# V's weights in one transfer ahead of the last block of x, and block 0's two V sums ahead of block 1's first, in a fused attention and gated MLP kernel

## The chip, the cores and the metric

The kernel runs on one core of a Trainium2 chip. The metric is the device time of one execution in microseconds (us). It is given as the median of several runs; the profile comes from one further execution, whose own time stands beside its span.

A core has five engines with a queue of instructions each: TensorE (PE in the profile: matrix products and transposes, results into the accumulation memory PSUM; PEld is its weight load), VectorE (DVE), ScalarE (ACT), GpSimd (POOL) and SyncE (SP), which here only issues transfers. Every engine takes its own instructions in order; between engines, semaphores make one wait for another. Transfers run on 16 DMA engines that all queues share.

## What is computed

One layer over 2048 rows of width 640 in bf16: a layer norm, whose result feeds both a sliding window attention (32 heads of 20, window 256) and a gated MLP of width 1536; both results are added to the input.

```python
def _A_ref(x, wqkv, wo):
    H = 32; Dh = D // H; W = 256
    qkv = ((x @ wqkv).reshape(B, S, 3, H, Dh)).transpose(2, 0, 3, 1, 4)
    q, k, v = qkv[0], qkv[1], qkv[2]
    scores = jnp.einsum("bhqd,bhkd->bhqk", q, k) * (Dh ** -0.5)
    mask = (idx[:, None] - idx[None, :] >= 0) & (idx[:, None] - idx[None, :] < W)
    p = _softmax(jnp.where(mask[None, None], scores, -1e9), axis=-1)
    o = jnp.einsum("bhqk,bhkd->bhqd", p, v)
    return o.transpose(0, 2, 1, 3).reshape(B, S, D) @ wo

def _B_ref(x, w_gate, w_up, w_down):
    h = _sigmoid(x @ w_gate) * (x @ w_up)
    return h @ w_down

xn = _layernorm(x)
return x + _A_ref(xn, A_wqkv, A_wo) + _B_ref(xn, B_w_gate, B_w_up, B_w_down)
```

## The kernel before

The 2048 rows are four chunks (c = 0 to 3) of 512, and a chunk is four blocks (s) of 128 rows. Width 640 is five slices (d) of 128. For a chunk the kernel needs xnT, the normalized rows turned so that the 640 features lie on the partitions; from it come Q and K (L324), V (L353), and gate and up (L447, L454).

The order of the work is written out by hand: each engine runs what the program issues to it, in that order. The change lies in the opening, which handles chunk 0 block by block, in two places, and in one later load.

**The loads at the top (L162 to L169).** SyncE issues, in this order: rows of block 0, 1 and 3 of x (`load_rows`, 160 KB each), the first half of V's weights (`load_v(0)`, columns 0 to 319 of 640, 400 KB in runs of 640 bytes), block 2 of x, the second half of V's weights, then Q's and K's weights (`load_wqkv`, 800 KB each in runs of 1280 bytes). Behind them on the same queue come the first gate and up weights (L183 on). The tiles of Q's and K's weights have six slices, of which `load_wqkv` fills 1 to 5, since a later step packs them into 0 to 4; V's tile has five. `load_wqkv` is called for Q and K alone, so its `1:` is fixed.

**The normalization of chunk 0.** Blocks 0 and 3 take their statistics on VectorE (`ln_half`, `ln_mv`, L252 and L258), the root on ScalarE (`root`, L644), and `norm` on VectorE (L648, L271). Blocks 1 and 2 take mean and root on ScalarE (`mean_act` L654, `root_act` L659 and L660) and the rest on VectorE (`norm_act`, L664 and L665).

**The transposes.** `transpose_rows(s, copy)` (L277) turns the five slices of a block on TensorE and copies them out of PSUM into xnT (L278): block 0 in two pieces on ScalarE, the others in one piece on VectorE.

**The V sums.** `project_v(c, s, hf)` (L353) is five products, one per slice, of a block's xnT with one half (hf) of V's weights, 128 by 320 out. In the code v01 is block 0, half 1, and v10 block 1, half 0. `copy_v` (L362) casts a sum into the V tile in two pieces of 64 rows. The order on TensorE is: transposes of 0; `keep_busy` of 512 and 128 columns; transposes of 1; v00; v10; transposes of 3; v01; v11; v30; transposes of 2; v31; v20; v21; then Q's and K's projections (`g_qk(0)`). `keep_busy` (L226) multiplies constants into a PSUM tile that nobody reads.

**The down weights.** `load_wd` (L195) loads w_down's twelve slices in five transfers: three, three, two, two and two slices. It is called while TensorE works on chunk 0's gate and up, behind the loads `turn_wo` (L205) and ahead of the stores of chunk 1's Q and K (L332), on SyncE's queue.

Everything after the opening is a fill order computed when the program is built: attention steps of a chunk with gate, up, Q, K, V, down and output work of this and the next chunk between them. The change leaves that order alone.

Of the kernel before, what the change touches and what calls it, by code (L numbers as in the profile page):

```python
# [9 lines left out]
P = 128  # L10
S = 2048
D = 640
# [4 lines left out]
FC = F // P  # L17
CW = 512
# [7 lines left out]
HALF = 320  # L26
# [67 lines left out]
def kernel(  # L94
# [11 lines left out]
    nc = tc.nc  # L106
# [35 lines left out]
    wqkv = [const.tile([P, DC + (part != "v"), D], BF16, name="w" + part) for part in "qkv"]  # L142
    wqkv_r = A_wqkv.rearrange("(c p) n -> p c n", p=P)
# [4 lines left out]

    ones = nc.const_aps.tensor(1.0, [P, CW], BF16)
    def load_wqkv(part):  # L150
        nc.sync.dma_start(out=wqkv[part][:, 1:, :], in_=wqkv_r[:, :, part * D:(part + 1) * D])

    xc[0] = xp.tile([P, SBC, D], BF16, name="xc")

    def load_rows(s, queue):
        queue.dma_start(out=xc[0][:, s, :], in_=xr[:, s, :])  # L156

    def load_v(hf):
        a = hf * HALF
        nc.sync.dma_start(out=wqkv[2][:, :, a:a + HALF], in_=wqkv_r[:, :, 2 * D + a:2 * D + a + HALF])  # L160

    load_rows(0, nc.sync)  # L162
    load_rows(1, nc.sync)
    load_rows(3, nc.sync)
    load_v(0)
    load_rows(2, nc.sync)
    load_v(1)
    load_wqkv(0)
    load_wqkv(1)  # L169

    scratch = {w: tc.dram_tile([H * 32, CW], BF16, name="s" + w) for w in "qk"}
# [22 lines left out]

    def load_wd():  # L195
        wd_r = B_w_down.rearrange("(c p) d -> p c d", p=P)
        for lo, hi in ((0, 3), (3, 6), (6, 8), (8, 10), (10, FC)):
            nc.sync.dma_start(out=wd[:, lo:hi, :], in_=wd_r[:, lo:hi, :])

    wo_i = tc.dram_tile([HG, NG * DH, D], BF16, name="wo_i")  # L200
# [22 lines left out]
    def keep_busy(widths):  # L223
        ps = ps_d.tile([P, CW], FP32, name="pwarm", tag="d")
        for n in widths:
            nc.tensor.matmul(ps[:, 0:n], lhsT=ones[:, 0:P], rhs=ones[:, 0:n], start=True, stop=True)  # L226
# [22 lines left out]
    def ln_half(c, s, a, stats=None):  # L249
        if a == 0:  # L250
            stats = lnp.tile([P, 2, nc.vector.BN_STATS_DIM], FP32, name="stats")
        nc.vector.bn_stats(out=stats[:, a, :], in_=xc[c][:, s, a * HALF:(a + 1) * HALF])  # L252
        return stats

    def ln_mv(stats, mv=None):
        if mv is None:
            mv = lnp.tile([P, nc.vector.BN_AGGR_DIM], FP32, name="mv")
        nc.vector.bn_aggr(out=mv, in_=stats)  # L258
        return mv
# [14 lines left out]
    def transpose_rows(s, copy, lo=0, hi=DC):  # L274
        pt = ps_h.tile([P, DC, P], BF16, name="pt", tag="h")
        for d in range(lo, hi):
            nc.tensor.transpose(pt[:, d, :], xns[0][:, s, d * P:(d + 1) * P], ident)  # L277
        copy(out=xnT[0][:, lo:hi, s * P:(s + 1) * P], in_=pt[:, lo:hi, :])  # L278
# [71 lines left out]
    def project_v(c, s, hf, home=ps_d, tag="d"):  # L350
        ps = home.tile([P, CW], FP32, name="pv", tag=tag)
        for d in range(DC):
            nc.tensor.matmul(ps[:, 0:HALF], lhsT=xnT[c][:, d, s * P:(s + 1) * P],  # L353
                             rhs=wqkv[2][:, d, hf * HALF:(hf + 1) * HALF],
                             start=(d == 0), stop=(d == DC - 1))
        return ps
# [285 lines left out]
    def root(mv):  # L642
        r = lnp.tile([P, 1], FP32, name="rstd")
        nc.scalar.activation(out=r, in_=mv[:, 1:2], func=SQRT, bias=eps)  # L644
        return r
# [17 lines left out]
    def norm_act(s, xn, neg, r):  # L663
        nc.vector.reciprocal(r, r)  # L664
        nc.vector.tensor_scalar(out=xn, in0=xc[0][:, s, :], scalar1=neg[:, 0:1],  # L665
                                scalar2=r[:, 0:1], op0=ADD, op1=MULT)
# [11 lines left out]
    stats3 = ln_half(0, 3, 0)  # L678
    for lo, hi in ((0, 3), (3, DC)):
        transpose_rows(0, act, lo, hi)  # L680
    keep_busy((CW, P))
    norm_act(1, xn1, neg1, r1)
    mv3 = ln_mv(ln_half(0, 3, 1, stats3))
    transpose_rows(1, dve)
    v00 = project_v(0, 0, 0)
    r3 = root(mv3)
    xn2, neg2 = mean_act(2)
    r2 = root_act(2, xn2, neg2)
# [1 line left out]
    v10 = project_v(0, 1, 0)  # L690
    copy_v(0, 0, 0, v00, dve, (0,))
    transpose_rows(3, dve)
    v01 = project_v(0, 0, 1)
    norm_act(2, xn2, neg2, r2)
    copy_v(0, 0, 0, v00, act, (1,))
    copy_v(0, 1, 0, v10, act)
# [32 lines left out]
    fill.add("x2", later(load_x, 2), 0)  # L729
    fill.add("wo_i", later(turn_wo), 0)  # L730
    fill.add("wd", later(load_wd), 0)
    fill.add("qk1", mix(g_qk(1), norms2, 6, 1, False), 50 * MM)
    fill.add("v1", mix(g_v(1), g_gu(1, 0, 2), 1, 2), 40 * 136 + 2 * GU)
# [111 lines left out]
```

## Time and profile before

| what | before |
|---|---|
| median of 3 runs | 308.35 us (308.08 to 308.82) |
| the profiled execution's own time | 308.19 us |
| its span | 306.5 us |
| granted TensorE clock, mean | 1.00 |
| TensorE busy / VectorE / ScalarE / GpSimd | 299.8 / 177.6 / 198.5 / 177.6 us |
| last share of x's blocks 0, 1, 3, 2 landed | 3.14, 3.56, 4.47, 7.35 us |
| last share of V's first half, second half landed | 6.89, 8.47 us |
| last share of Q's and K's weights landed | 10.69, 12.97 us |
| first V sum / first Q product starts | 6.94 / 13.01 us |

Times inside the span are counted from its start. A transfer counts as landed when the last of the 16 DMA engines has reported its share; the trace keeps these reports, and no printed view shows them. In the profile's lines "xn<-xc" reads "writes xn from xc", "x5" is the number of instructions merged into the line, and the name after the engine is the source line. Starts of products are recorded and their ends are modelled, so two neighbouring lines can overlap a little; the chain of waits, followed back from the last instruction, counts a group from the moment it took over.

### The profile page before, as it was taken

What the parts mean: (1) busy time and instruction counts of PE and PEld (TensorE: products, weight loads), DVE (VectorE), ACT (ScalarE), POOL (GpSimd) and SP (SyncE); (2) the same over time, 40 slices, a digit from 0 to 9 for tenths busy, and PEclk for the clock granted to TensorE, in tenths of its full rate; (3) what the DMA queues carried; (4) which work ended last, traced back from release to release, by engine and by line L of the source; (5) the groups of instructions that cost most, each with busy time, mean ns of one, the idle gap of its engine ahead of it and who ended that gap; (6) DMA issues with size and microseconds to landing.
All of it is one profiled execution on the core that took longest, in us unless ns stands there. A gap on an engine that the chain in (4) does not pass through costs nothing.

```text
span 306.5 us, 9993 instructions
## 1 busy us (share of the span) xinstructions
PE 299.8 (98%) x4279; PEld 164.9 (54%) x4314; DVE 177.6 (58%) x355; ACT 198.5 (65%) x197; POOL 177.6 (58%) x317
## 2 busy tenths in 40 slices
PE   7999999999999999999999999999999999999996
PEld 3654444445657654554557654554546665444775
DVE  5735539879675564496946464483733626372433
ACT  6923877698854649888674647878585547778000
POOL 3174687687982927676682728557382847557000
PEclk9999999999999999999999999999999999999999
DMA  7997987986427052810046212740000210000202
GB/s 204 362 326 255 305 202 214 316 243 217 144 91 170 21 180 70 256 58 2 2 132 130 66 58 83 242 137 0 2 2 2 69 42 25 2 2 2 88 21 68
DMA packets 40174, 36.87 MB, mean 120 GB/s; under 512 B 8992, under 2 KB 39840, under 8 KB 40096
## 3 DMA queue, kind: packets, MB, share of 16 engines
q1 hardware_dynamic: 39264, 35.45, 38.1%
q10 hardware_dynamic: 864, 0.77, 0.9%
q8 instruction: 34, 0.56, 0.7%
q14 instruction: 12, 0.10, 0.1%
HBM read 25.59 MB, written 11.44 MB: 121 GB/s over the span
## 4 chain that ended last, share of the span: by engine, by line
PE 96%; issue 1%; DMA 1%; ACT 1%; DVE 0%; SPq 0%
PE y L468 18%; PE pu L454 17%; PE pg L447 17%; PE pqk L324 14%; PE ps L524 9%; PE pv L353 8%; PE y L475 7%; PE acc L557 6%; DMA xc<-in_A_x_dram 1%; PE pt L277 0%; ACT xn L654 0%; ACT xn L659 0%; DVE xn L665 0%; SPq L156 0%; ACT rstd L660 0%
## 5 line engine op out<-in xcount | busy, mean ns | idle before, releaser
L541 POOL TENSOR_SCALAR_AFFINE_SELECT pT<-pT 64x512 bf16<-64x512 bf16 (+1 forms) x256 | 157.3, 614 | 83.0 <-ACT pT L530 70.6
L530 ACT ACTIVATE pT<-ps 128x2048 bf16<-128x2048 f32 (+1 forms) x76 | 141.0, 1855 | 59.5 <-PE ps L524 52.9
L458 DVE SCALAR_TENSOR_TENSOR h<-th,pu 128x512 bf16<-128x512 f32 x48 | 32.7, 681 | 49.7 <-PE pu L454 44.2
L454 PE MATMUL pu<-xnT,wu 128*128 128x512 bf16 x228 | 59.0, 380 | 0.7 <-issue 0.2
L447 PE MATMUL pg<-xnT,wg 128*128 128x512 bf16 x226 | 58.5, 380 | 0.9 <-issue 0.3
L468 PE MATMUL y<-wd,h 128*128 128x320 bf16 (+2 forms) x396 | 56.6, 295 | 0.0
L468 PEld LDWEIGHTS <-h 128*128 128x128 bf16 x396 | 36.8, 98 | 15.6 <-issue 1.8
L450 ACT ACTIVATE th<-pg 128x512 f32<-128x512 f32 x48 | 28.6, 595 | 15.5 <-PE pg L447 15.4
L447 PEld LDWEIGHTS <-wg 128*128 128x128 bf16 x240 | 22.3, 98 | 25.8 <-issue 2.0
L454 PEld LDWEIGHTS <-wu 128*128 128x128 bf16 x240 | 22.0, 98 | 25.5 <-issue 2.0
L524 PE MATMUL ps<-qT,kT 20*64 20x320 bf16 (+4 forms) x1440 | 32.1, 260 | 0.0
L569 DVE STREAM_TRANSPOSE t<-acc 128x512 f32<-128x512 f32 x32 | 21.1, 697 | 17.2 <-PE acc L557 17.2
L524 PEld LDWEIGHTS <-kT 20*64 20x64 bf16 x1440 | 15.4, 103 | 25.0 <-issue 22.4
L479 DVE SCALAR_TENSOR_TENSOR rows<-y,rows 128x320 bf16<-128x320 f32 x30 | 14.5, 488 | 22.5 <-PE y L475 22.4
L581 DVE TENSOR_TENSOR on<-t,rec 128x320 bf16<-128x320 f32 (+4 forms) x48 | 25.9, 540 | 1.1
L353 PE MATMUL pv<-wv,xnT 128*128 128x320 bf16 x160 | 25.8, 300 | 0.0
L475 PE MATMUL y<-wo,oc 128*128 128x320 bf16 (+2 forms) x165 | 24.2, 295 | 0.0
L324 PE MATMUL pqk<-xnT,wk 128*128 128x512 bf16 x97 | 23.0, 380 | 0.2
L324 PE MATMUL pqk<-xnT,wq 128*128 128x512 bf16 x94 | 22.7, 380 | 0.4 <-issue 0.2
L362 DVE CAST v<-pv 64x320 bf16<-64x320 f32 x29 | 14.1, 486 | 11.8 <-PE pv L353 11.6
L557 PE MATMUL acc<-pT,v 64*32 64x320 bf16 (+4 forms) x1440 | 19.7, 253 | 0.0
L557 PEld LDWEIGHTS <-v 64*32 64x32 bf16 x1440 | 16.2, 91 | 5.8 <-issue 1.6
(53 smaller groups left out, 194.8 us busy)
## 6 DMA issues: line engine op xcount, KB each, us to landing
qT<-sq SPq DMA_DIRECT2D x16, 256.0 KB
kT<-sk SPq DMA_DIRECT2D x16, 256.0 KB
sq<-st SPq DMA_DIRECT2D x20, 128.0 KB
sk<-st SPq DMA_DIRECT2D x20, 128.0 KB
out_dram<-rows SPq DMA_DIRECT2D x15, 160.0 KB
wg<-in_B_w_gate_dram SPq DMA_DIRECT2D x4, 480.0 KB
wu<-in_B_w_up_dram SPq DMA_DIRECT2D x4, 480.0 KB
xc<-in_A_x_dram SPq DMA_DIRECT2D x3, 640.0 KB
```

Of the source, the lines that this page charges most:

```text
L324: nc.tensor.matmul(ps, lhsT=wt[:, m, :], rhs=xnT[c][:, d, :], start=(d == 0), stop=(d == DC - 1))
L353: nc.tensor.matmul(ps[:, 0:HALF], lhsT=xnT[c][:, d, s * P:(s + 1) * P], rhs=wqkv[2][:, d, hf * HALF:(hf + 1) * HALF], start=(d == 0), stop ...
L447: nc.tensor.matmul(pg, lhsT=part(wg, d, f), rhs=xnT[c][:, d, :], start=(d == 0), stop=(d == DC - 1))
L450: nc.scalar.activation(out=th, in_=pg, func=TANH, scale=0.5)
L454: nc.tensor.matmul(pu, lhsT=part(wu, d, f), rhs=xnT[c][:, d, :], start=(d == 0), stop=(d == DC - 1))
L458: nc.vector.scalar_tensor_tensor(out=h, in0=th, scalar=1.0, in1=pu, op0=ADD, op1=MULT)
L468: nc.tensor.matmul(y[:, 0:cut[1] - cut[0]], lhsT=ht[c, f][:, s * P:(s + 1) * P], rhs=wd[:, f, cut[0]:cut[1]], start=(f == 0), stop=False)
L475: nc.tensor.matmul(y[:, 0:cut[1] - cut[0]], lhsT=oc[c, m][:, s * P:(s + 1) * P], rhs=wo[:, m, cut[0]:cut[1]], start=False, stop=(m == DC - 1))
L524: nc.tensor.matmul(ps[a * U:(a + 1) * U, i, col * U:(col + n) * U], lhsT=qk["k", kc, o // GH][32 * i:32 * i + DH, o % GH + a, kb * U:(kb + ...
L530: nc.scalar.activation(out=pt[:, :, 0:width], in_=ps[:, :, 0:width], func=EXP, scale=SCALE)
L541: nc.gpsimd.affine_select(out=view, in_=view, pattern=[[0, HG], [0, n], [sign, U]], compare_op=GE, fill=0.0, base=base, channel_multiplier ...
L557: nc.tensor.matmul(acc[32 * i:32 * i + 32, q * U:(q + n) * U], lhsT=vt[kb][a * U:(a + 1) * U, u, h * VW:h * VW + 32], rhs=pt[a * U:(a + 1) ...
```

## The change

V's weights come in one transfer of 800 KB, in runs of 1280 bytes, issued where their first half was, ahead of block 2 of x; the second transfer goes, and `load_v` with it. `load_wqkv` now serves V too, whose tile it fills from slice 0. `keep_busy` after block 0's transposes has 384 columns in one product instead of 640 in two. v00 stands ahead of the transposes of block 1, and v01 right behind them, ahead of v10. w_down is loaded in six transfers of two slices each. No other instruction is added or removed.

```diff
     def load_wqkv(part):
-        nc.sync.dma_start(out=wqkv[part][:, 1:, :], in_=wqkv_r[:, :, part * D:(part + 1) * D])
+        nc.sync.dma_start(out=wqkv[part][:, int(part < 2):, :], in_=wqkv_r[:, :, part * D:(part + 1) * D])
...
-    def load_v(hf):
-        a = hf * HALF
-        nc.sync.dma_start(out=wqkv[2][:, :, a:a + HALF], in_=wqkv_r[:, :, 2 * D + a:2 * D + a + HALF])
...
     load_rows(3, nc.sync)
-    load_v(0)
+    load_wqkv(2)
     load_rows(2, nc.sync)
-    load_v(1)
     load_wqkv(0)
     load_wqkv(1)
...
-        for lo, hi in ((0, 3), (3, 6), (6, 8), (8, 10), (10, FC)):
+        for lo, hi in ((0, 2), (2, 4), (4, 6), (6, 8), (8, 10), (10, FC)):
             nc.sync.dma_start(out=wd[:, lo:hi, :], in_=wd_r[:, lo:hi, :])
...
-    keep_busy((CW, P))
+    keep_busy((3 * P,))
     norm_act(1, xn1, neg1, r1)
     mv3 = ln_mv(ln_half(0, 3, 1, stats3))
+    v00 = project_v(0, 0, 0)
     transpose_rows(1, dve)
-    v00 = project_v(0, 0, 0)
+    v01 = project_v(0, 0, 1)
     r3 = root(mv3)
...
     transpose_rows(3, dve)
-    v01 = project_v(0, 0, 1)
     norm_act(2, xn2, neg2, r2)
```

## The prediction

> **What bounds the kernel.** First the page's busy time by engine and the chain that ended last, by engine.
>
> ```profile
> PE 299.8 (98%) x4279; PEld 164.9 (54%) x4314; DVE 177.6 (58%) x355; ACT 198.5 (65%) x197; POOL 177.6 (58%) x317
> ...
> PE 96%; issue 1%; DMA 1%; ACT 1%; DVE 0%; SPq 0%
> ```
>
> TensorE works in 98% of the 306.5 us span and is 96% of the chain. So the question is what the change does to TensorE's own row of work. The waits of TensorE hold three entries with another engine or a queue behind them: 0.8 us before its first instruction, 0.5 and 0.4 us ahead of the first two groups of transposes; the rest is "issue". After 6.5 us nothing makes it wait, so what the opening loses or wins arrives at the end one for one. Next the chain in order of time, there (start us, us, what):
>
> ```profile
> 5.99 0.46 DVE xn L665
> 6.44 0.05 issue
> 6.49 0.45 PE pt L277 x5
> 6.94 1.51 PE pv L353 x10
> 8.45 0.28 PE pt L277 x5
> 8.73 2.04 PE pv L353 x15
> 10.77 0.28 PE pt L277 x5
> 11.05 2.12 PE pv L353 x15
> 13.17 0.22 PE pqk L324
> ```
>
> Block 1's normalized rows come at 6.44, then TensorE runs without a gap: transposes of 1, two V sums, transposes of 3, three sums, transposes of 2, three sums, Q. One detail: a group of transposes costs 0.28 us, but the first stands at 0.45. The V sum behind it could have started at 6.77 and started at 6.94. The landing records of the trace (each of the 16 DMA engines reports its share; no view prints them) say why: the last share of V's first half came at 6.89. **V's weights are already last there.** So I read the opening's timeline (start us, us, engine, line, operation):
>
> ```profile
> 2.18 0.43 SPq L160 DMA_DIRECT2D wv<-in_A_wqkv_dram  x1
> ...
> 2.66 0.52 SPq L156 DMA_DIRECT2D xc<-in_A_x_dram  x1
> ...
> 3.22 0.43 SPq L160 DMA_DIRECT2D wv<-in_A_wqkv_dram  x1
> ...
> 5.64 0.44 PE L226 MATMUL pwarm<-const-bfloat16-1.0 128*128 128x512 bf16 x2
> 5.73 0.75 ACT L278 COPY xnT<-pt 128x384 bf16<-128x384 bf16 x2
> ...
> 7.00 0.48 DVE L278 COPY xnT<-pt 128x640 bf16<-128x640 bf16 x1
> ...
> 7.37 0.74 ACT L654 ACTIVATE xn<-xc 128x640 bf16<-128x640 bf16 x1
> ```
>
> The two halves are issued 1.04 us apart with x's block 2 between. The windows' DMA share is 0.89 at 3 to 4 us, 0.81 at 4 to 5, then 1.09, 1.06, 1.01, 1.05: from 5 us the DMA engines have no room, and a byte put ahead of another delays it.
>
> **When V is there.** Last landings before: x block 3 at 4.47, V's first half 6.89, x block 2 7.35, V's second half 8.47, wq 10.69, wk 12.97. Now all 800 KB must land before block 0's first V sum, although that sum reads only one half: one transfer, one wait.
> Late bound: the slowest engine keeps its pace and only x block 2 leaves from in front: 8.47 - (7.35 - 6.89) = 8.01.
> Early bound: the pace of wk, an equal transfer with as long rows: engine means of wq and wk are 10.09 and 12.37, so 2.28 us. From x block 3's mean, 4.01, plus 0.30 for the idle shares (1 - 0.89, 1 - 0.81), plus wq's slowest behind its mean, 0.60: 7.19.
> Neither is nearer in kind: the late bound has the place in the queue, the early one the shape. I take the middle, **L = 7.6 us**.
>
> A rule of the Trainium skill points earlier (DMA: Bandwidth & Descriptors, "Rules for kernel authors" and the fixed cost under "Anatomy of one DMA"): coalesce small transfers, since each carries some 2 us of fixed cost. By it, as an estimate, V would land 2 us ahead of the late bound, near 6.0. The trace disagrees: V's second half came 1.12 us behind x block 2 on the slowest engine, half of wq's 2.22, so a queued transfer showed no such fixed part.
>
> **The change part by part.**
> (1) Sum v00 moves ahead of the transposes of block 1. Its other input, block 0's xnT, is copied by 6.48 (5.73 + 0.75), so V decides: start at L + 0.05 (the lag seen at 6.89/6.94) = 7.65 instead of 6.94: +0.71.
> (2) TensorE takes instructions in order, so the transposes of block 1, ready at 6.44, now queue behind v00. They were done ahead of the first V sum and now stand behind it: +0.28.
> (3) Who waits for these: VectorE's copy of block 1 (it began 0.51 after its transposes began, took 0.48), behind it on VectorE block 3's reciprocal and normalization (0.16 + 0.45) and the rest. Counting from L: v00 0.05 to 0.73, transposes of 1 to 1.01, v01 to 1.69, copy of 1 done 1.72, v10 to 2.42; block 3 normalized 2.39; its transposes 2.42 to 2.70; VectorE's cast of half of v00 2.39 to 2.87; copy of 3 done 3.42; v11 to 3.38, so v30 waits some 0.06; block 2's transposes from 4.12. Its x lands at L + 0.46, ScalarE needs 2.14 from there (7.37 to 9.51), VectorE comes to it after the copy of 3 and has it at 4.07: in time by 0.05. v31 to 5.08; copy of 2 done 5.12; v20 waits 0.06. So v01, taken early, covers the copy of block 1, and what is left is +0.12, bounds 0 and 0.4 (a block normalized 0.3 late).
> (4) keep_busy loses 256 columns, 0.11 us by the spacing of 0.22 for 512: nothing, since TensorE then idles for V. Without that idle it would be the -0.11 of the rival below.
> (5) One V issue less on SyncE (0.43): wq and wk go out earlier, but the DMA engines are full and both are needed after 13 us, landed 10.69 and 12.97: nothing.
> (6) w_down in six transfers instead of five, same bytes. SyncE issues them at 53.30 to 56.93 and the Q stores from 57.35 stand behind. One more issue is 0.37 to 0.77 (that line's shortest and longest). Block 1's spreads read those stores; the four pairs of issues end at 75.18, and block 1's first scores come about 81.95; w_down's first reader is at 82.3. Covered by several us: nothing; uncovered, 0.4 to 0.8.
>
> Sum: +0.71 + 0.28 + 0.12 = **+1.11 us**, or L - 6.49. With L at its bounds and (3) at its own: 7.19 - 6.61 = +0.58 up to 8.01 - 6.61 + 0.4 = +1.80. The profiled execution took 308.19 (span 306.5 and 1.7 around it): 309.30. It stands 0.16 below the median of the runs: **309.45**.
>
> **Rivals.**
> *V whole is in time (not slower).* If the longer rows or the single transfer keep the slowest engine from its lag, L is the fastest engine's: 5.45 + 1.13 (its second half behind x block 2: 5.99 to 7.12) = 6.58. V's wait then ends 0.1 after the copy at 6.48 and the gaps at 6.0 to 6.9 are filled by v00: 6.58 - 6.49 = +0.09, and 308.45. If V came still earlier the sum's first three products could start on the first copy, about 6.12, and the run end 0.4 earlier, 307.95. It decides from L below 7.1. For it: the landing spread of 1.44 in V's first half (5.45 to 6.89) may belong to its short rows; wk's is 1.13. Against: it asks the slowest engine to gain over 0.9 us, and spreads over 1.1 stay through wq and wk. With the runs' scatter some of this would read as faster.
>
> *TensorE falls to a lower clock.* It idles from about 5.85 to 7.65. That the array starts slow is seen in this trace though the granted clock reads 1.00: the weight loads of keep_busy at 2.07, 2.50, 2.93, 3.35 are 0.43 apart, later ones 0.22, after some 3.4 us of work. Falling back would cost half of such a stretch, 1.7: 309.45 + 1.7 = 311.15. For it: an idle time four times any after the start. Against: transposes and keep_busy stand right before it, and gaps of 0.46 and 0.41 did nothing. The skill's page (TensorE: Matmul & The Clock Gate, "Why this matters for your kernels") sets the limit at idle gaps of about 3 us; by it 1.8 would be safe and this rival starts only with a wait past 9 us. No run here shows such a gap.
>
> *The sixth w_down transfer is felt.* If block 1's spreads come late in spite of the cover, 0.4 to 0.8 more: near 310.1.
>
> **How the numbers follow.** Chances: forecast 0.70, V in time 0.20, lower clock 0.07, w_down 0.03. The time is the forecast's, **309.45**; its own range is +0.58 to +1.80, 308.9 to 310.15. The range asked for reaches down into the rival of V in time (its +0.09 to +0.58) and leaves out its low end and the lower clock: **308.6 to 310.2**. A measurement here can tell about 0.2%, 0.62 us, from no change. Slower by more: the forecast but for its lowest end (0.64), clock and w_down (0.10): 0.74. Within: the lowest end of the forecast (0.06) and most of the rival (0.14): 0.20. Faster: 0.06, from the rival's 307.95 and scatter.
>
> **What would show it.** Right: TensorE idle about 1.8 us after the second keep_busy, ended by V's weights or named "issue"; v00 near 7.65; V's last landing 7.2 to 8.0 and x block 2's about 0.46 behind; the first Q product near 14.1 instead of 13.01; the chain passing through a V transfer instead of x's block 1; past 14 us the same sequence, shifted. Wrong: v00 starting at 6.5, or a Q start at 13.1 or earlier (V in time); spacings of 0.43 in the first Q products (clock); a first block 1 score shifted by more than Q is (w_down).

## The result, and the profile after

| what | before | changed |
|---|---|---|
| median of 15 runs | 308.20 us (308.08 to 308.82) | 311.76 us (309.53 to 313.97) |
| ratio of the times | | 1.0112, 95% interval 1.0084 to 1.0140 |
| the profiled execution's own time / span | 308.19 / 306.5 us | 310.62 / 308.8 us |
| mean granted TensorE clock, 15 runs of the changed kernel | | 1.00 in 6 runs (309.53 to 311.01), 0.987 to 0.995 in 9 runs (311.64 to 313.97) |
| V's last share landed | 8.47 us (second half) | 8.18 us (whole) |
| first V sum / first Q product starts | 6.94 / 13.01 us | 8.22 / 14.73 us |

The change makes the kernel slower, by 3.6 us in the median against the 1.1 us that were forecast, and its times, which agreed within 0.8 us before, now spread over 4.4 us. The profiled execution is one of the six at full clock, so its trace shows only a part of this. (Lines of the changed kernel below 162 of the old numbering stand five lower: the V sums are L348.) First the page's busy times and the shares of its chain:

```profile
PE 299.5 (97%) x4278; PEld 164.7 (53%) x4313; DVE 177.3 (57%) x355; ACT 198.5 (64%) x197; POOL 177.0 (57%) x317
...
PE 94%; DMA 2%; ACT 1%; issue 1%; POOL 1%; SPq 0%; DVE 0%
```

TensorE does the same work in a longer span, and a transfer has entered the chain. The chain in order of time says which (start us, us, what):

```profile
2.13 0.04 issue
2.18 6.00 DMA wv<-in_A_wqkv_dram
8.18 0.04 issue
8.22 0.84 PE pv L348 x5
9.06 0.28 PE pt L272 x5
9.34 1.44 PE pv L348 x10
10.78 0.28 PE pt L272 x5
11.06 1.44 PE pv L348 x10
12.50 0.28 PE pt L272 x5
12.78 2.12 PE pv L348 x15
14.90 0.22 PE pqk L319
```

Before, the chain ran through x's block 1, ScalarE and VectorE. Now it is SyncE, V's transfer for 6 us, and from 8.22 TensorE without a gap. Behind the first V sum stand the transposes of block 1 that used to be done ahead of it. The waits of TensorE (us in total, times, longest) hold it in two lines:

```profile
PE pv L348 <- DMA wv<-in_A_wqkv_dram: 2.2, 1, 2.2
...
PE ps L519 <- ACT pT L525: 0.2, 1, 0.2
```

The first is the opening: Q starts 1.72 us later. The second is a new wait near 48 us, 0.24 us, of which the prediction said nothing. These two make 1.97 us, and every instruction of ScalarE and VectorE from 60 us to the end stands later by just that. The rest of the span's 2.3 us, 0.35, lies behind VectorE's last instruction, in the stores: 2.69 us from that instruction's end to the span's end, 2.34 before.

### The profile page after: what moved, and what is told of

Read it like the earlier page. It is cut to its first block, busy times and chain, and to the rows that moved or that the text cites. A ratio compares the mean times of both kernels' runs of the same rounds, so it can differ in the third digit from the quotient of the medians.

```text
span 308.8 us, 9992 instructions
## 1 busy us (share of the span) xinstructions
PE 299.5 (97%) x4278; PEld 164.7 (53%) x4313; DVE 177.3 (57%) x355; ACT 198.5 (64%) x197; POOL 177.0 (57%) x317
## 4 chain that ended last, share of the span: by engine, by line
PE 94%; DMA 2%; ACT 1%; issue 1%; POOL 1%; SPq 0%; DVE 0%
PE y L463 17%; PE pu L449 16%; PE pg L442 16%; PE pqk L319 14%; PE ps L519 8%; PE pv L348 8%; PE y L470 7%; PE acc L552 6%; DMA wv<-in_A_wqkv_dram 2%; ACT pT L525 1%; POOL pT L536 1%; SPq L156 0%; PE pt L272 0%; ACT th L445 0%; DVE xn L474 0%
## 5 line engine op out<-in xcount | busy, mean ns | idle before, releaser
L348 PE MATMUL pv<-wv,xnT 128*128 128x320 bf16 x160 | 26.1, 300 | 2.2 <-DMA wv<-in_A_wqkv_dram 2.2
L357 DVE CAST v<-pv 64x320 bf16<-64x320 f32 x29 | 14.1, 485 | 11.8 <-PE pv L348 11.6
L348 PEld LDWEIGHTS <-xnT 128*128 128x128 bf16 x160 | 14.4, 98 | 11.2 <-issue 2.6
```

## Experiments

The theory after the result: two costs. One is the wait for all of V in every execution. The other comes in some executions only: TensorE, idle for over 2 us, is granted a lower clock afterwards. The rivals: the new order costs by itself, the sixth w_down transfer costs, the spread comes from V's landing, or the low clock is chance or belongs to one chip.

**The order alone** (transfers, and w_down, as before):

```diff
-    keep_busy((CW, P))
+    keep_busy((3 * P,))
...
+    v00 = project_v(0, 0, 0)
     transpose_rows(1, dve)
-    v00 = project_v(0, 0, 0)
+    v01 = project_v(0, 0, 1)
...
     transpose_rows(3, dve)
-    v01 = project_v(0, 0, 1)
```

> The kernel before with the changed order on TensorE alone (v00, transposes of block 1, v01, v10; 384 columns of keep_busy); V stays in two transfers around block 2 of x. Theory (the wait for V sets the opening, the order only decides which half is waited for): v00 starts at 6.94 as before, since its half lands at 6.89; v01 then waits for the second half, 8.47, instead of the 7.90 at which TensorE is ready; the first Q product near 14.1 (before 13.01), the run about 1.1 us over before, and TensorE's longest idle time near 1.1 us. If the longest idle time decides whether the clock falls, the mean granted clock stays 1.00 in every run. Rival (the order itself costs, whatever V does): Q near 14.7 and the same slow scatter of times as the changed kernel, 309.5 to 314.

Measured: 309.36 us (308.90 to 309.62, 8 runs), ratio 1.0030 (1.0020 to 1.0040), clock 1.00 in all. TensorE's timeline (start us, us, ... [idle before, what ended it]):

```profile
6.71 0.84 PE L353 MATMUL pv<-wv,xnT 128*128 128x320 bf16 x5 [0.72 <-DMA wv<-in_A_wqkv_dram]
7.39 0.44 PE L277 MATMUL pt<-ident,xn 128*128 128x128 bf16 x5
8.30 1.53 PE L353 MATMUL pv<-wv,xnT 128*128 128x320 bf16 x10 [0.47 <-DMA wv<-in_A_wqkv_dram]
```

As the theory said: each sum waits for its half, Q comes 0.78 later (13.79; 14.1 was expected, but V's second half landed at 8.26 here, not at 8.47), and the narrow spread stays. The 0.24 us near 47 us is here too, so it goes with the order, not with the transfer.

**The single transfer alone** (order, keep_busy and w_down as before):

```diff
-    load_v(0)
+    load_wqkv(2)
     load_rows(2, nc.sync)
-    load_v(1)
```

> The change's single V transfer alone, with the order, keep_busy and w_down of before (transposes of block 1 ahead of v00). Theory: v00 starts when V whole has landed, about 8.2, the transposes of block 1 are done before it and no longer behind it, so Q is at 8.2 + 6.07 = 14.3 against 14.73 in the changed kernel and 13.01 before; TensorE idles 1.3 us there instead of 2.2. If an idle time of 2.2 us is what lets the clock fall, this one keeps 1.00 in most runs and stands 1.3 us over before; if the clock falls here as well, the mean granted clock goes to 0.99 and the times above 311 in many runs. Rival (the order matters more than the load): the time of before within 0.3 us.

Measured: 309.72 us (309.24 to 313.43, 12 runs), ratio 1.0062 (1.0037 to 1.0088). The clock was 0.989 to 0.994 in 3 of 12 runs, and these three are the longest, 311.98 to 313.43; the other nine end at 310.43. In the profile, one at full clock, V landed at 7.84, and its first sum came then:

```profile
6.40 0.45 PE L272 MATMUL pt<-ident,xn 128*128 128x128 bf16 x5 [0.41 <-DVE xn L660]
7.88 1.52 PE L348 MATMUL pv<-wv,xnT 128*128 128x320 bf16 x10 [1.03 <-DMA wv<-in_A_wqkv_dram]
```

Q starts 0.94 late and no wait follows near 47 us. So the transfer alone costs 1.4 us in the median, against 3.6 for the whole change, and the clock falls at times without the new order. The three long runs were not profiled, so how long TensorE idled in them is not known.

**The changed kernel with work in the wait:**

```diff
-    keep_busy((3 * P,))
+    keep_busy((CW,) * 10)
```

> The changed kernel with ten products of 512 columns of keep_busy instead of one of 384 ahead of v00: same wait for V, but TensorE works through it (10 x 0.216 = 2.2 us from 5.65 to 7.85). Theory (the runs above 311 come from a clock that falls after the idle 2.2 us): the mean granted clock is 1.00 in all runs, the times lie between 309.5 and 311, the median about 1.9 us over before, and Q is still near 14.7. Rival (the spread comes from when V lands, or from later waits, not from the clock): the times spread from 309.5 to 314 as without the filler.

Measured: 310.97 us (310.06 to 311.72, 6 runs), ratio 1.0079 (1.0061 to 1.0096), clock 0.999 or 1.00 in all six. The runs near 314 are gone, which fits the clock as their cause; two of the six still end over 311. The median is 2.7 over before and not the 1.9 that were expected. In the profiled execution (311.01) V landed later still, at 8.85, which accounts for this one:

```profile
5.62 2.35 PE L221 MATMUL pwarm<-const-bfloat16-1.0 128*128 128x512 bf16 x10
8.89 0.84 PE L348 MATMUL pv<-wv,xnT 128*128 128x320 bf16 x5 [0.92 <-DMA wv<-in_A_wqkv_dram]
```

**w_down in six transfers alone:**

```diff
-        for lo, hi in ((0, 3), (3, 6), (6, 8), (8, 10), (10, FC)):
+        for lo, hi in ((0, 2), (2, 4), (4, 6), (6, 8), (8, 10), (10, FC)):
```

> The kernel before with w_down in six transfers of two slices, nothing else. Theory (the sixth issue is covered): the time of before within 0.2 us. Rival (it delays the stores of chunk 1's Q and K and what reads them): 0.4 to 0.8 us more, and a wait of TensorE for a transfer or for ScalarE between 45 and 85 us.

Measured: 308.42 us (308.23 to 309.06, 11 runs), ratio 1.0002 (0.9994 to 1.0011). No cost.

**The changed kernel once more**, unedited.

> The changed kernel once more, beside the three others of this job. Theory (an idle TensorE of 2.2 us lets its clock fall in some executions): about half the runs show a mean granted clock of 0.987 to 0.995 and times over 311.5, the others 1.00 and 309.5 to 311; if the profiled execution is one of the former, its granted clock by windows shows a stretch at half speed that begins after the wait for V and lasts 3.5 to 8 us. Rival (the low clock belongs to the chip of the first runs): 1.00 in all runs.

Measured: 312.32 us, 0.995 in 4 of 6 runs (312.26 to 312.96), 1.00 in two (310.27 and 310.43). The profiled execution (312.26, span 310.5) is one of the four:

```profile
8.30 1.49 PE L348 MATMUL pv<-wv,xnT 128*128 128x320 bf16 x5 [2.37 <-DMA wv<-in_A_wqkv_dram]
```

Its windows (start:end length, busy time and instructions of PE, PEld, DVE, ACT and POOL, then the granted clock, the DMA share and GB/s):

```profile
6.00:7.00 1.00, 0.00 (x0) 0.10 (x1) 0.96 (x3) 0.45 (x2) 0.00 (x0) 1.00 1.03 332
7.00:8.00 1.00, 0.00 (x0) 0.00 (x0) 0.04 (x1) 0.29 (x1) 0.00 (x0) 1.00 1.04 383
8.00:9.00 1.00, 0.69 (x3) 0.41 (x3) 0.00 (x0) 0.25 (x1) 0.00 (x0) 0.62 1.07 397
9.00:10.00 1.00, 1.00 (x7) 0.71 (x6) 0.00 (x0) 0.97 (x3) 0.00 (x0) 0.50 1.07 375
10.00:11.00 1.00, 1.00 (x8) 0.65 (x6) 0.59 (x3) 0.82 (x3) 0.00 (x0) 0.50 1.07 362
11.00:12.00 1.00, 1.00 (x7) 0.60 (x6) 0.81 (x2) 0.10 (x1) 0.00 (x0) 0.67 1.08 353
12.00:13.00 1.00, 1.00 (x12) 0.81 (x11) 0.28 (x1) 0.87 (x3) 0.00 (x0) 1.00 1.09 331
```

This is the second cost, seen. TensorE does nothing from 6 to 8 us, the clock reads 1.00 all that time, and as the V sums begin it drops to 0.50. A window at 0.62 was low for 0.76 us of it, one at 0.67 for 0.66: 0.76 + 1 + 1 + 0.66 = 3.4 us at half speed. The V sum that takes 0.84 in the first profile takes 1.49 here:

```profile
8.26 0.04 issue
8.30 1.49 PE pv L348 x5
9.80 0.53 PE pt L272 x5
10.33 2.07 PE pv L348 x10
```

V came at 8.26, within 0.1 us of the first profile, yet the work after the opening stands 3.35 us later than before instead of 1.73. Less 0.08 for the later V, the clock is worth 1.5 us in this execution. The low clock belongs to no single chip: the single transfer alone, this run and the kernel with v01 first, further down, ran on three.

**Two halves in the place of the whole** (the changed kernel with V's halves in two transfers, both ahead of block 2):

```diff
-    load_wqkv(2)
+    load_v(0)
+    load_v(1)
     load_rows(2, nc.sync)
```

> The changed kernel with V in two transfers of one half each, both ahead of block 2 of x: same bytes in the same place, but v00 waits for its half only. Theory (what costs is that the first sum waits for all 800 KB): first half landed near 6.9, v00 there, second half near 8.0, v01 near 8.05, Q near 13.6 (+0.6 on before), 0.2 more from the wait near 47 us that the changed order showed, so some 309.1; TensorE idles 1.1 us at most and the clock stays 1.00 in all runs. Rival (one transfer of long rows lands no later than two halves, the place ahead of block 2 is what costs): block 2, landing near 8.5, holds the opening as it does in the changed kernel, Q near 14.5.

Measured: 309.29 us (309.04 to 309.69, 6 runs), ratio 1.0030 (1.0018 to 1.0042), clock 1.00 in all.

```profile
6.43 0.84 PE L353 MATMUL pv<-wv,xnT 128*128 128x320 bf16 x5 [0.48 <-DMA wv<-in_A_wqkv_dram]
7.11 0.44 PE L277 MATMUL pt<-ident,xn 128*128 128x128 bf16 x5
7.77 1.53 PE L353 MATMUL pv<-wv,xnT 128*128 128x320 bf16 x10 [0.22 <-DMA wv<-in_A_wqkv_dram]
```

The halves landed at 6.39 and 7.73, Q started at 13.46, and block 2, landed at 8.18, held nothing. Same bytes, same place, same order as in the changed kernel, and 3 us less in the median: what costs is that the first sum waits for all 800 KB. One difference besides stays open: the rows are 640 bytes again, and all of V was there at 7.73, against 7.84 to 8.85 with V whole in six profiles. On the mean of the 16 engines the whole is hardly later (6.93 to 7.24 against 7.10); its slowest engine is.

**The changed kernel without the second keep_busy** (`keep_busy((3 * P,))` deleted):

> The changed kernel without the 384 columns of keep_busy: TensorE idles 0.2 us longer ahead of v00 and has less work before it. Theory (the idle time decides whether the clock falls): a mean granted clock under 1.00 in at least as many runs as in the changed kernel, two thirds or more, median 312 or above; in the runs at 1.00 the time is the changed kernel's, 309.5 to 311. Rival (the clock falls by chance, whatever stands there): the same share as the changed kernel or less, with no shift of the median.

Measured: 312.16 us (310.42 to 313.96), the clock under 1.00 in 5 of 6 runs; the profiled execution idled 2.55 us and shows the same stretch at 0.50.

```profile
8.36 1.49 PE L348 MATMUL pv<-wv,xnT 128*128 128x320 bf16 x5 [2.55 <-DMA wv<-in_A_wqkv_dram]
```

The median did not move from the 312.32 of the changed kernel beside it, and 5 of 6 against 13 of 21 is too close to tell, so this run does not separate the two rivals.

**One more ScalarE instruction in the kernel before:**

```diff
     nc.scalar.activation(out=scr, in_=eps, func=SQRT)
+    nc.scalar.activation(out=scr, in_=eps, func=SQRT)
```

> The kernel before with one more ScalarE instruction of 0.2 us at about 3.0 us, where ScalarE is idle until 3.58. The changed order makes the compiled ScalarE queue one instruction longer before 47 us (63 recorded against 62), and there an exponential (L530) starts 0.3 us late with nothing named that explains it. Theory (the queue's own next stretch of instructions arrives there, and one more instruction moves the point ahead of that exponential): the same late start near 45 to 46 us, TensorE 0.24 us later from there, 308.5 to 308.6. Rival (the late start comes from the order on TensorE): nothing changes, within 0.1 us of before.

Measured: 308.49 us (308.37 to 309.00, 11 runs), ratio 1.0009 (1.0001 to 1.0018). Three ScalarE timelines at the same exponential: before, changed, and this one.

```profile
46.06 1.88 ACT L530 ACTIVATE pT<-ps 128x2048 bf16<-128x2048 f32 x1 [0.87 <-PE ps L524]
```

```profile
48.12 1.88 ACT L525 ACTIVATE pT<-ps 128x2048 bf16<-128x2048 f32 x1 [1.20 <-POOL pT L536]
```

```profile
46.29 1.88 ACT L531 ACTIVATE pT<-ps 128x2048 bf16<-128x2048 f32 x1 [1.18 <-POOL pT L542]
```

The idle time before it grows by 0.3 us in the third as in the second, and TensorE is held the same 0.2 us, though here the order on TensorE is that of before:

```profile
PE ps L525 <- ACT pT L531: 0.2, 1, 0.2
```

GpSimd is named because it came last by the profile; the wait on it is the same in all three programs. So one instruction more in ScalarE's queue suffices. The changed order adds one, since a copy there has to wait for two engines instead of one. All twelve traces agree: with 63 ScalarE instructions ahead of this exponential it follows 1.18 to 1.20 us of idle time, with 62 it follows 0.87. Why stays open. A fetch of the queue's next instructions at that spot would fit, but it is not shown: an 8 KB transfer of an instruction queue begins within 0.8 us of this exponential's start in every trace, whether it is late or not. On the Trainium skill's page Runtime: NRT & Kernel Launch, "Instruction fetch mechanics", the next block is fetched while the current one runs and the cost is mostly hidden; no run here shows whether the 0.2 us are such a cost.

**Idle time without any change to the transfers** (the kernel before, v01 ahead of v00, so that the first sum needs V's second half):

```diff
     transpose_rows(1, dve)
+    v01 = project_v(0, 0, 1)
     v00 = project_v(0, 0, 0)
...
     transpose_rows(3, dve)
-    v01 = project_v(0, 0, 1)
```

> The kernel before with all its transfers and its transposes of block 1 first, but v01 ahead of v00: the first V sum now needs V's second half, which lands at 8.2 to 8.8 in the profiles so far, so TensorE idles about 1.5 us there with no transfer changed. Theory (idle time of TensorE alone lets the clock fall, the more often the longer): a mean granted clock of 0.987 to 0.995 in more than the 3 of 12 runs that 1.0 us of idle time gave and fewer than the 13 of 21 of the changed kernel; the other runs at about 1.5 us minus the 0.1 that the order saves over before, 309.6 to 309.9. Rival (the single large transfer has a part in it): 1.00 in all runs.

Measured: 310.64 us (309.49 to 311.70, 6 runs), ratio 1.0068 (1.0046 to 1.0090); the clock was 0.994 in 3 of 6 runs, the three longest. In the profiled one, 311.69, TensorE idled 1.64 us ahead of the sum:

```profile
8.58 3.87 PE L353 MATMUL pv<-wv,xnT 128*128 128x320 bf16 x15 [1.64 <-DMA wv<-in_A_wqkv_dram]
```

Its windows:

```profile
7.00:8.00 1.00, 0.00 (x0) 0.00 (x0) 0.96 (x4) 0.89 (x3) 0.00 (x0) 1.00 1.03 317
8.00:9.00 1.00, 0.42 (x3) 0.27 (x3) 0.08 (x1) 0.97 (x4) 0.00 (x0) 0.85 1.02 364
9.00:10.00 1.00, 1.00 (x5) 0.58 (x4) 0.00 (x0) 0.37 (x2) 0.00 (x0) 0.50 1.06 392
```

The single transfer is not needed for the clock to fall; the idle time is.

**Half of the filler** (the changed kernel with `keep_busy((CW,) * 5)`):

> The changed kernel with five products of 512 columns of keep_busy (1.08 us) instead of one of 384: TensorE idles about 1.5 us of the wait for V instead of 2.3. Theory (the length of the idle time decides how often the clock falls): a lower share of runs under 1.00 than the 18 of 27 of the kernels with 2.2 us or more, and a higher one than the 0 of 6 with 0.9 us; the runs at 1.00 lie where those of the changed kernel lie, 309.5 to 311. Rival (any work in the wait, or none, makes no difference): two thirds of the runs under 1.00.

Measured: 311.36 us (310.34 to 312.10, 6 runs), ratio 1.0098 (1.0082 to 1.0113), the clock 0.999 or 1.00 in all. The share I expected between the two ends did not show, but neither did the idle time: V landed at 7.95 in the profile, and TensorE idled only 0.88 us:

```profile
7.99 0.84 PE L348 MATMUL pv<-wv,xnT 128*128 128x320 bf16 x5 [0.88 <-DMA wv<-in_A_wqkv_dram]
...
PE pu L449 <- issue: 0.7, 2, 0.5
```

Most of the times lie above those of the changed kernel at full clock (309.53 to 311.01), and the profile shows a cause for a part: an "issue" wait of TensorE of 0.5 us near 207 us that no other profile here has, and behind it the work stands 0.7 us later. What that wait is stays open.

Over all kernels, by the idle time ahead of the first V sum in their profiles. The third column is explained below the table.

| kernel | idle us ahead of the sum | most idle in one stretch of 3.41 us, opening | runs with the clock under 0.999 |
|---|---|---|---|
| before / w_down alone / one ScalarE instruction more | none / 0.28 / none | 0.87 / 1.23 / no record | none |
| two halves / order alone | 0.48 / 0.72 | 1.02 / 1.35 | 0 of 6 / 0 of 8 |
| half filler / full filler | 0.88 / 0.92 | 0.88 / 0.81 | 0 of 6 / 0 of 6 |
| single transfer alone | 1.03 | 1.22 | 3 of 12 |
| v01 first | 1.64 | 2.05, fell | 3 of 6 |
| changed, first profile and second | 2.24 and 2.37 | 1.72, and 2.40, fell | 13 of 21 |
| changed, no second keep_busy | 2.55 | 2.62, fell | 5 of 6 |

The length of the wait does not say why one execution of the changed kernel falls and another does not, with waits of 2.37 and 2.24 us. The traces do: they keep each change of the granted clock, which no printed view lists. In eleven of the twelve (one has no record) the changes stand whole multiples of 3.413 us apart, and the first comes at another moment in each, between 3.49 and 5.88 us. Cut from there into stretches of 3.413 us, all eleven give one rule, with idle times from the profile's modelled ends. The clock fell at the end of each of the thirteen stretches with 2.01 us or more of idle time that end inside a trace (three in openings, ten around or behind the last product), and at the end of none with 1.77 or less. In the second profile of the changed kernel one stretch, from 4.83 to 8.24, holds the whole wait. In the first a border at 6.91 cuts it, and the clock stays. So the chance lies in where the borders fall; no run here sets them. As an estimate from these numbers, a wait of 2.3 us leaves 2.0 us in one stretch for (3.41 - 2.3 + 2 x 0.3) / 3.41 of the positions, or half; 13 of 21 were counted.

## Why the prediction was wrong

**What bounds the kernel, and that V is last: right.** Whatever the opening lost reached the end, one for one; the chain now passes through V's transfer, and v00 begins 0.04 us behind its landing.

**The sum's form: right.** It said that Q moves by L - 6.49. The profile gives 8.18 - 6.49 = 1.69, measured 1.72; from v00 to Q it is 6.51 us against 6.07 before, so the transposes and the small waits came to 0.44 where 0.28 + 0.12 were put.

**L: wrong in size.** I took 7.6 with bounds of 7.19 and 8.01, and four of six executions passed the late one. The profiles of five runs with V whole have 7.84, 8.18, 8.26, 8.32 and 8.85; with the half filler, 7.95. The early bound failed twice: it put the mean of the DMA engines at 6.59, and it was 6.93 to 7.24; and it put the slowest 0.60 us behind the mean, as for Q's weights in one trace, and it was 0.90 to 1.60. V's first shares came at 6.56 to 6.68 in all six, at the 6.58 that I had for the fastest engine, and the last ones 1.2 to 2.3 us later. Both bounds were built from one execution's lag, and that lag varies. The rival "V whole is in time" asked for no lag at all and never came near. The Trainium skill's rule on coalescing (DMA: Bandwidth & Descriptors, "Rules for kernel authors"), from which I estimated an L near 6.0, is not borne out either. Its section "Anatomy of one DMA", with the 2 us of fixed cost, is about transfers that GpSimd issues; these come from SyncE, so it was weak ground.

**The lower clock: the step that failed most.** I gave it 0.07 and kept its 1.7 us out of the sum and the range, on the ground that gaps of 0.46 and 0.41 us had done nothing. That says nothing about 2.2 us: those gaps leave 0.87 us idle in one stretch, the wait for V whole up to 2.62. Its price was right: 1.7 by the pace of the first keep_busy products, 1.5 measured. With 13 of 21 runs in it, the median is that rival's: it forecast 311.15, and 311.76 was measured. One reading was wrong beside it: the 1.00 of the windows during the slow first products is no reading, as the trace has no record of the clock ahead of 4.15 us. The rule set beside it, the Trainium skill's TensorE: Matmul & The Clock Gate, "Why this matters for your kernels" (no idle gaps over about 3 us), is not enough for these runs: the clock fell behind waits of 1.64, 2.37 and 2.55 us in three traces. The length of the low stretch, 3.4 us, does agree with the window of about 3.4 us that the Trainium skill states on that page, in Part 1, for the change of state.

**keep_busy at nothing: half right.** It hid behind V's wait, as said; but work in that wait was what would have held the clock, and the full filler shows it.

**SyncE's issue and w_down at nothing: right** (1.0002 for w_down; Q's and K's weights landed at 10.87 and 13.15, Q starts at 14.73).

**What I did not have:** the 0.24 us near 48 us.

Put together, the median of the changed kernel is 3.6 us over before: 1.7 for V, 0.24 for the late exponential, some 1.5 for the clock, by the two profiles. What stays open: why the stores' end lies up to 0.6 us further behind VectorE's last instruction in some traces, which engine lags in V's transfer and why, and what the runs at 0.987 to 0.989 (313.4 to 314.0) look like inside; at the same arithmetic they would hold two stretches at half speed, but none of them was profiled. No variant came out faster than the kernel before.

## What to carry to other kernels

Before two transfers become one, ask which product reads which part first: one transfer is one wait, and the wait ends with the slowest DMA engine. When a wait moves onto TensorE, price the idle time twice, once as itself and once as the slower clock that may follow, and judge by many runs, since one profile shows one of the two outcomes. Where such a wait can't be avoided, constant products in it kept the clock here (0 of 12 runs low, against 13 of 21). That they cost nothing is not shown: the two kernels with them have medians of 311.0 and 311.4 us, the eight runs of the changed kernel at full clock one of 310.3, and the traces explain the difference only in part.

## What the runs showed of the hardware

TensorE's granted clock fell to 0.50 for 3.41 us in three profiled executions, behind waits of 1.64, 2.37 and 2.55 us. In eleven traces it changed only at borders that stand whole multiples of 3.413 us apart: to 0.50 behind each stretch with 2.01 us or more of idle time, and behind none with 1.77 or less. It does not need work to fall: in the kernel before it fell at 307.94 us, 4.1 us behind the last product. No kernel with a wait of 0.92 us or less in its profile had a run at the lower clock (0 of 26 with 0.48 to 0.92). A load of 800 KB over 16 DMA engines ended on its fastest engine between 6.56 and 6.68 us in six executions, and on its slowest between 7.84 and 8.85. One instruction more in ScalarE's queue, 0.2 us long and in idle time, delayed an exponential 43 us later by 0.3 us.
